# A dynamic convolution ahead of a feed-forward layer: its matmuls cut from 128 rows to two row halves of 64

## The chip, the cores and the metric

The kernel runs on one core of one Trainium2 chip. The metric is the device time of one execution in microseconds (us); less is better. A time is given as the median of several runs. The profile is of one further execution.

## The reference

```
B, S, D = 8, 4096, 192;  H, K = 8, 7;  group = D // H          # 24 channels a head
w = softmax(weight_gen, axis=-1)                               # [B, S, H, K]
x_pad = concatenate([zeros(B, K - 1, D), x], axis=1)
conv[b, s, h, g] = sum_k w[b, s, h, k] * x_pad[b, s + k, h, g] # causal, 7 taps, per token and head
h = maximum(conv.reshape(B * S, D) @ w_in, 0)                  # [32768, 192] @ [192, 2048]
out = (h * h) @ w_out                                          # [32768, 2048] @ [2048, 192], float32
```

Each token and head has seven weights of its own, which mix the token's row of `x` with the six rows before it. The result passes through a feed-forward layer with a squared ReLU.

## The kernel before, in words

**Tiling.** Tokens are taken in 64 subblocks of 512 (`TB`), eight to a batch. Subblocks are grouped in `BLOCKS`: the first two blocks have one subblock each, and all others two, which makes 33 blocks, numbered from 0. Two subblocks of a block are its two halves. The main loop (L858 to L893) runs over the blocks. In the loop for block j it computes the feed-forward layer's first matrix for block j, the second for the blocks before it, and the conv for block j + 1.

**Softmax.** Class `Softmax` (L190 to L279) turns `weight_gen` into normalized weights `v_big`, eight slots a token and head, of which seven hold the taps. `store` writes them to a DRAM tile `vd`. `wr_load` (L341) reads them back on SP's DMA queue, one row per input token of a conv piece, and `x_load` (L323) brings the rows of `x` on POOL's DMA queue. Both go through `block_load` (L307), in which a subblock has `NT` = 5 pieces of 128 input rows, one each `STEP` = 104 output tokens; the first and the last subblock of a batch part have a piece that is loaded on its own.

**Bands.** The conv is a matmul with a banded matrix. `st_bands` (L649) and `st_band` (L385) make it on VectorE: the row's weights `wr`, repeated, times a 0/1 `mask` (L115, made by POOL at the start) give `bd`, with 4160 elements a partition for a subblock.

**Conv.** From the ninth block on (`FIRST_SPREAD` = 8), `st_conv_spread` (L472) runs it. The result for 192 channels lies in `y` as slots of 64 partitions per half: each slot has two heads of 24 channels, at partitions 0 and 32 of the half, and in the remaining 8 partitions of each 32 a share of the last two heads. For four slots, five pieces, two halves and two heads of a slot it issues one matmul (L493): 128 input rows contract to 32 channels by 104 tokens (96 in the last piece). The 32 channels go to one of four column strips of the array (`tile_position=(0, p0)`), so that four matmuls in a row use four strips. That is 80 matmuls a block, into two PSUM tiles `yp`; ACT copies the first, VectorE the second to `y` (L503). The fourth slot (index `NK` = 3) holds the last two heads; four DMAs on SP (L507) move them into the free 8 partitions of the other slots. The conv before the ninth block is `st_conv` (L509, matmuls L527) or `st_conv_first` (L435).

**Feed-forward.** `st_unit` (L562) is one of 16 units of a block: three slots times two halves of 64 rows, in pairs, make `h` (L572); ACT applies the ReLU (L586), VectorE squares (L590). `st_mm2` (L602, matmul L621) multiplies with `w_o`, in pairs of 64 rows; ACT and VectorE add the two halves (`o_sum`, L635 and L637), and SP stores the rows (L642). `load_w_spread` (L143) puts the rows of `w_in` in the order in which the channels lie in `y`.

**Order.** The order on each engine is the program's order, written out by hand. A plan string per block sets it: for blocks whose successor is the ninth or a later one it is

```
steady_spread = "MuMuuu" * 2 + "MuCMuuu" + "MuMuuu"
```

with `u` a unit, `M` half a quarter of the second matrix, `C` the conv of the next block, followed by the `x` loads of the block after that. Bands for the next block are put at units 1 and 5. `h` and `yp` share a ring of three PSUM buffers (`ps_h`, two banks each). At the start (L689 to L733) POOL builds the mask (L692), issues loads, and clears `v_big` (L733); its next work is the `x` load of the fourth subblock and its share of the early `wr` loads (L355), which feed the bands for the first conv of L527.

Of the kernel before, what the change touches and what calls it, by code (L numbers as in the profile page):

```python
# [9 lines left out]
def kernel(  # L10
# [26 lines left out]
    nc = tc.nc  # L37
    f32 = mybir.dt.float32
    f16 = mybir.dt.float16

    B, S, D = x.shape
    H, KK = weight_gen.shape[2], weight_gen.shape[3]
# [3 lines left out]
    G = D // H  # L46
    SPREAD = H - 2
    FIRST_SPREAD = 8
    HP = H // 2

    P = 128
    TB = 512
    NBB = S // TB
    NSUB = B * NBB
    BLOCKS = [(0, 1), (1, 1)] + [(n, 2) for n in range(2, NSUB, 2)]
# [6 lines left out]
    SL = 8  # L62
    RT = 64
    NK = D // RT

    NT = 5
    STEP = 104
    BASE = -24
    starts = [BASE + STEP * i for i in range(NT)]
    bounds = [0, 104, 208, 312, 416, TB]  # L70
    ROW_ORDER = (0, 1, 2, 3, 4)

    AluOp = mybir.AluOpType
    AxisX = mybir.AxisListType.X
# [2 lines left out]
    const = ctx.enter_context(tc.tile_pool(name="const", bufs=1))  # L77
# [5 lines left out]
    p_bd = ctx.enter_context(tc.tile_pool(name="p_bd", bufs=3))  # L83
# [12 lines left out]
    w_p = const.tile([P, WQ, 2, NQ + NQ // 2], f16, name="w_p")  # L96
    w_o = const.tile([P, NF, Dm], f16, name="w_o")
    mask = const.tile([P, P, 2], f16, name="mask")
    FIRST = 8
    NSEL = TB + TB - P + FIRST - 1 + P  # L100
    sel = const.tile([P, NSEL], f16, name="sel")
    PARTS = {0: (8, 8, 8, 8), 1: (8, 8, 16), 2: (16, 16)}
    v_big = const.tile([P, R + 2 * HALO, HP, SL, 2], f16, name="v_big")
    v_first = [
        const.tile([P, FIRST + 2 * HALO, HP, SL, 2], f16, name=f"v_first{i}") for i in (0, 1)
    ]
# [18 lines left out]

    x_st = {}

    def load_w_in(dst, q, eng):  # L130
# [12 lines left out]
    def load_w_spread():  # L143

        def rows(head, k=None):
            a = moe_w_in[G * head : G * (head + 1)]
            return a if k is None else a.rearrange("(r k) c -> k r c", k=NK)[k]

        for e in (0, 1):
            for k in range(NK):  # L150
                for a, n, src in (
                    (0, G, rows(2 * k + e)), (G, RT // 2 - G, rows(SPREAD + e, k))
                ):
                    if k < 2:
                        p0 = RT * k + 32 * e + a
                        nc.gpsimd.dma_start(
                            out=w_p[p0 : p0 + n, :, 0, 0:NQ],
                            in_=src.rearrange("r (q c) -> r q c", q=WQ),
                        )
                    else:  # L160
                        for half in (0, 1):
                            p0 = RT * half + 32 * e + a
                            nc.gpsimd.dma_start(
                                out=w_p[p0 : p0 + n, :, 0, NQ:],
                                in_=src.rearrange("r (q h c) -> h r q c", q=WQ, h=2)[half],
                            )
# [23 lines left out]
    class Softmax:  # L190
# [35 lines left out]
        def exp(self, lo, hi):  # L226

            if lo == 0:
                self.ex = self.tile(p_one, p_one, "ex", HK, "ex8").rearrange(
                    "p (r g k e) -> p r g k e", g=HP, k=KK, e=2  # L230
                )
# [22 lines left out]
        def scale(self, lo, hi, eng):  # L254

            v = self.v
            while lo < hi:
                n = min(SL - lo % SL, hi - lo)
                for g in range(HP):
                    eng.tensor_tensor(  # L260
# [20 lines left out]
    vd_t = {}  # L281
# [7 lines left out]
    x_t, wr_t, pr_t, bd_t, yp_t, y_t, g_t, gp_t, t1_t, o_t, o_sb_t = ({} for _ in range(11))  # L289

    def rows(ap2d, t0, width):

        return bass.AP(
            tensor=ap2d.tensor, offset=ap2d.offset + t0 * width,
            ap=[[width, P], [STEP * width, NT], [1, width]],
        )
# [5 lines left out]
    def tile_start(j, i):  # L302

        t1 = (j % NBB + 1) * TB
        return TB - P if i == NT - 1 and t1 in ends(j // NBB) else starts[i]

    def block_load(j, dst, src, width, eng):  # L307
        t0 = (j % NBB) * TB
        first, last = int(t0 == 0), NT
        if first:  # L310
            eng.dma_start(out=dst[:, 0], in_=src[0:P, :])  # L311
        a = t0 + tile_start(j, NT - 1)
        if a != t0 + starts[-1]:
            last = NT - 1
            eng.dma_start(out=dst[:, last], in_=src[a : a + P, :])
        ap = rows(src, t0 + starts[first], width)
        ap = bass.AP(
            tensor=ap.tensor, offset=ap.offset,
            ap=[ap.ap[0], [STEP * width, last - first], ap.ap[2]],
        )  # L320
        eng.dma_start(out=dst[:, first:last], in_=ap)  # L321

    def x_load(j):  # L323
        x_t[j] = p_x.tile([P, NT, D], f16, name="xt")
        block_load(j, x_t[j], x[j // NBB], D, nc.gpsimd)

    def x_load_f32(j):
# [13 lines left out]
    def wr_load(j):  # L341
        wr_t[j] = p_wr.tile([P, NT, HP, SL * 2], f16, name="wr")
        wr = wr_t[j].rearrange("p t g c -> p t (g c)")
        block_load(j, wr, vd_t[j // NBB], H * SL, nc.sync)

    def wr_load_sbuf(j, parts, order, engines):
# [38 lines left out]
    def st_band(j, tiles):  # L385


        if j not in bd_t:
            bd_t[j] = p_bd.tile([P, H * NT * STEP], f16, name="bd")
        i = tiles[0]  # L390
        lo = STEP * i
        shift = 0 if i == 0 and j % NBB == 0 else lo - tile_start(j, i)
        n = min(STEP, P - shift)
        shape = (P, HP * len(tiles), n // SL, 2 * SL)
        nc.vector.tensor_tensor(  # L395
            out=bd_t[j][:, H * lo : H * (lo + len(tiles) * n)].rearrange(
                "p (g m c) -> p g m c", g=shape[1], c=2 * SL
            ),
            in0=wr_t[j][:, i : tiles[-1] + 1]
            .rearrange("p t g c -> p (t g) c")  # L400
            .unsqueeze(2)
            .broadcast_to(shape),
            in1=mask[:, shift : shift + n]
            .rearrange("p (m c) e -> p m (c e)", c=SL)
            .unsqueeze(1)
            .broadcast_to(shape),
            op=AluOp.mult,
        )

# [62 lines left out]
    def st_conv_spread(j):  # L472

        s0, n = BLOCKS[j]
        y = p_y.tile([P, NK + 1, TB], f16, name="y")
        y_t[j] = y
        for ks in ((NK, NK - 1), (0, 1)):
            yp = ps_h.tile([P, 2, TB], f32, name="yp", tag="h")
            k0 = min(ks)
            for k in ks:  # L480
                for i in range(NT):
                    a, b = bounds[i], bounds[i + 1]
                    for half in (0, 1):
                        s = s0 + half
                        hi = a + (STEP if tile_start(s, i) == starts[i] else b - a)
                        bd = bd_t[s][:, H * a : H * hi].rearrange(
                            "p (g c e) -> p g e c", g=HP, e=2
                        )
                        for e in (0, 1):
                            head = 2 * k + e  # L490
                            p0 = RT * half + 32 * e
                            c0 = min(G * head, D - 32)
                            nc.tensor.matmul(  # L493
                                out=yp[p0 : p0 + 32, k - k0, a:b],
                                lhsT=x_t[s][:, i, c0 : c0 + 32],
                                rhs=bd[:, head // 2, e, 0 : b - a],
                                start=True,
                                stop=True,
                                skip_group_check=True,
                                tile_position=(0, p0),  # L500
                            )
            copy = nc.vector.tensor_copy if k0 == 0 else nc.scalar.copy
            copy(out=y[:, k0 : k0 + 2], in_=yp)  # L503
        for p0 in range(0, P, 32):
            head = SPREAD + p0 // 32 % 2
            r0 = p0 + G * head - min(G * head, D - 32)
            nc.sync.dma_start(out=y[p0 + G : p0 + 32, 0:NK], in_=y[r0 : r0 + G, NK])  # L507

    def st_conv(j):  # L509

# [136 lines left out]
        )  # L647

    def st_bands(j):  # L649
        first = int(j % NBB == 0)  # L650
        last = NT - int(tile_start(j, NT - 1) != starts[-1])
        split = 2 if j == BLOCKS[NFIRST][0] else first
        for tiles in (range(first), range(first, split), range(split, last), range(last, NT)):
            if tiles:
                st_band(j, tiles)

    with nc.allow_low_precision("fp16 matmul pipeline"), tc.manual_schedule():
# [3 lines left out]
        for b in range(B):  # L661
            t0 = 0
# [68 lines left out]
        s2.load(nc.gpsimd)  # L731
        x_load(2)
        nc.gpsimd.memset(v_big, 0.0)  # L733

# [12 lines left out]
        fill = {}  # L749
# [22 lines left out]
        for n, s in enumerate(parts):  # L772
            k = n - min(m for m, p in enumerate(parts) if p.b == s.b)
# [4 lines left out]
        for n, s in enumerate(parts[4:], 4):  # L778
            b, f = s.b, s.fb
            k = n - min(m for m, p in enumerate(parts) if p.b == b)  # L780
# [8 lines left out]
        for j in range(len(plans), NBLK - 1):  # L789
            a = BLOCKS[j + 1][0]  # L790
# [67 lines left out]
        for j in range(NBLK):  # L858
# [6 lines left out]
            for step in plans[j].split():  # L865
                kind, n = step[0], int(step[1:] or 0)
# [29 lines left out]
        j = NBLK - 1  # L896
# [44 lines left out]
```

The softmax here doesn't subtract the row's maximum and nothing guards it: scores larger than these inputs give would overflow.

## Time and profile before

| what | us |
|---|---|
| median of three runs | 732.07 (731.87 to 732.11) |
| the profiled execution | 731.82 |
| its span, from the first to the last instruction | 730.0 |
| PE, matmuls busy | 724.1 |
| VectorE busy | 626.8 |
| ACT busy | 612.2 |
| POOL busy | 99.8 |
| the conv matmuls of L493, 2000 of them, in 25 convs | first at 155.2, last at 686.4 |

The granted TensorE clock is 1.0 through the whole span. Shares in the profile are of the span. A group's row gives the line, the engine, the operation, what is written from what, the shapes (partitions x elements), the count, then busy us and mean ns of one, and the idle time before them with what ended it. Matmuls overlap one another, so their busy times say less than the distance of their starts.

### The profile page before, as it was taken

The numbers are of one execution on the slowest core, as the hardware profiler recorded it, in microseconds if no ns is written. First come the engines' busy times: TensorE is split into PE (matmuls) and PEld (weight loads), VectorE is DVE, ScalarE is ACT, GpSimd is POOL, SyncE is SP. The second block draws the span as 40 slices with busy tenths as digits, with TensorE's granted clock in tenths as the row PEclk, the third lists the DMA queues.
The fourth block names the chain that finished last, engine by engine and source line by source line (L and its number), as shares of the span: only waits on it lengthen the run. The fifth ranks groups of instructions, "written<-read, shape, count | busy, mean of one in ns | idle before, by whom it ended". The sixth has DMA issues, their size and how long they took to land.

```text
span 730.0 us, 30988 instructions
## 1 busy us (share of the span) xinstructions
PE 724.1 (99%) x14053; PEld 528.0 (72%) x14053; DVE 626.8 (86%) x836; ACT 612.2 (84%) x733; POOL 99.8 (14%) x145
## 2 busy tenths in 40 slices
PE   8999999999999999999999999999999999999998
PEld 4657788777777777777777777777777777777777
DVE  7998998998898988888988888988889988778753
ACT  5999888888888888888888888888888888888883
POOL 8131223321001100011001010010000110001000
PEclk9999999999999999999999999999999999999999
DMA  9555455685345452455432554343544325444012
GB/s 202 118 105 115 82 96 105 132 149 129 86 66 138 90 92 59 82 117 124 76 64 61 136 104 88 56 77 116 107 84 86 57 52 119 66 87 78 30 45 68
DMA packets 125984, 68.30 MB, mean 94 GB/s; under 512 B 85321, under 2 KB 122140, under 8 KB 125340
## 3 DMA queue, kind: packets, MB, share of 16 engines
q0 software_dynamic: 46192, 19.43, 22.9%
q1 hardware_dynamic: 79516, 46.79, 22.4%
q8 instruction: 110, 1.80, 1.1%
q14 instruction: 22, 0.18, 0.1%
q10 hardware_dynamic: 144, 0.10, 0.0%
HBM read 50.18 MB, written 28.70 MB: 108 GB/s over the span
## 4 chain that ended last, share of the span: by engine, by line
PE 98%; ACT 1%; DVE 0%; DMA 0%; issue 0%
PE o L621 47%; PE h L572 44%; PE yp L493 4%; PE h L557 2%; PE yp L527 1%; DMA wg<-in_weight_gen_dram 0%; PE yp L455 0%; ACT y L538 0%; DVE v_first L260 0%; PE pr L372 0%; ACT t L586 0%; DVE ssum L245 0%; ACT ex L238 0%; DVE rcp L252 0%; ACT wr L381 0%
## 5 line engine op out<-in xcount | busy, mean ns | idle before, releaser
L586 ACT ACTIVATE t<-h 128x1024 f16<-128x1024 f32 x512 | 496.4, 1026 | 60.3 <-PE h L572 58.8
L621 PEld LDWEIGHTS <-g 64*128 64x128 f16 (+1 forms) x8032 | 344.3, 94 | 55.0 <-issue 2.2
L621 PE MATMUL o<-w_o,g 64*128 64x192 f16 (+1 forms) x8032 | 380.1, 243 | 0.1
L590 DVE TENSOR_TENSOR g<-t 128x2048 f16<-128x2048 f16 (+1 forms) x287 | 307.4, 1105 | 30.1 <-ACT t L586 29.9
L572 PE MATMUL h<-y,w_p 64*128 64x512 f16 x2400 | 291.7, 376 | 0.0
L572 PEld LDWEIGHTS <-w_p 64*128 64x128 f16 x2400 | 113.9, 94 | 94.7
L395 DVE TENSOR_TENSOR bd<-wr,mask 128x4160 f16<-128x4160 f16 (+4 forms) x90 | 149.6, 1686 | 1.3 <-ACT wr L381 0.7
L637 DVE TENSOR_TENSOR o_sb<-o,o_sb 128x384 f32<-128x384 f32 x123 | 68.4, 556 | 61.1 <-ACT o_sb L635 60.1
L321 POOL DMA_DIRECT2D xt<-in_x_dram x63 | 52.6, 839 | 415.3 <-PE yp L493 362.5
L635 ACT COPY o_sb<-o 128x384 f32<-128x384 f32 x129 | 61.6, 477 | 45.9 <-PE o L621 45.1
L572 PE MATMUL h<-y,w_i 64*128 64x512 f16 x576 | 70.6, 376 | 0.3 <-ACT t L586 0.3
L572 PEld LDWEIGHTS <-w_i 64*128 64x128 f16 x576 | 30.3, 94 | 22.2 <-issue 1.6
L493 PEld LDWEIGHTS <-xt 128*32 128x32 f16 x2000 | 24.6, 95 | 10.6 <-issue 10.6
L260 DVE TENSOR_TENSOR v_big<-ex,rcp 128x112 f16<-128x112 f32 (+5 forms) x180 | 29.9, 237 | 1.7 <-DMA vd<-v_big 0.7
L503 DVE CAST y<-yp 128x1024 f16<-128x1024 f32 x25 | 30.4, 1218 | 0.0
L493 PE MATMUL yp<-bd,xt 128*32 128x104 f16 (+1 forms) x2000 | 28.4, 210 | 0.0
L238 ACT ACTIVATE ex<-wg 128x560 f32<-128x560 f32 (+4 forms) x38 | 25.9, 682 | 1.9 <-DMA wg<-in_weight_gen_dram 1.9
L245 DVE TENSOR_REDUCE ssum<-ex 128x80 f32<-128x560 f32 (+4 forms) x38 | 25.3, 666 | 1.3 <-ACT ex L238 1.3
L503 ACT CAST y<-yp 128x1024 f16<-128x1024 f32 x25 | 25.2, 1007 | 0.0
L252 DVE RECIPROCAL rcp<-ssum 128x80 f32<-128x80 f32 (+4 forms) x38 | 22.8, 600 | 1.3
L311 POOL DMA_DIRECT2D xt<-in_x_dram x7 | 3.9, 554 | 120.9 <-PE yp L493 109.4
L355 POOL DMA_DIRECT2D wr<-v_first x24 | 12.9, 560 | 25.1 <-DVE v_first L260 13.6
(41 smaller groups left out, 115.1 us busy)
## 6 DMA issues: line engine op xcount, KB each, us to landing
out_dram<-o_sb SPq DMA_DIRECT2D x63, 384.0 KB
xt<-in_x_dram POOLq DMA_DIRECT2D x42, 240.0 KB, 4.7
wg<-in_weight_gen_dram SPq DMA_DIRECT2D x4, 1064.0 KB
xt<-in_x_dram POOLq DMA_DIRECT2D x21, 192.0 KB, 5.2
wr<-vd SPq DMA_DIRECT2D x38, 80.0 KB
vd<-v_big SPq DMA_DIRECT2D x5, 512.0 KB
y<-y SPq DMA_DIRECT2D x100, 24.0 KB
wg<-in_weight_gen_dram SPq DMA_DIRECT2D x3, 616.0 KB
```

What stands on the lines that cost most here:

```text
L238: nc.scalar.activation(out=self.ex[:, lo:hi].rearrange("p r g k e -> p (r g) k e"), in_=self.wg[:, lo:hi].rearrange("p r (g e) k -> p (r g ...
L260: eng.tensor_tensor(out=bass.AP(tensor=v.tensor, offset=v.offset + lo * H * SL + lo % SL * 2 + g * SL * 2, ap=[list(v.ap[0]), [H * SL + 2, ...
L321: eng.dma_start(out=dst[:, first:last], in_=ap)
L395: nc.vector.tensor_tensor(out=bd_t[j][:, H * lo : H * (lo + len(tiles) * n)].rearrange("p (g m c) -> p g m c", g=shape[1], c=2 * SL), in0= ...
L493: nc.tensor.matmul(out=yp[p0 : p0 + 32, k - k0, a:b], lhsT=x_t[s][:, i, c0 : c0 + 32], rhs=bd[:, head // 2, e, 0 : b - a], start=True, sto ...
L503: copy(out=y[:, k0 : k0 + 2], in_=yp)
L572: nc.tensor.matmul(out=h[:, half], lhsT=w_in_chunk(w, u, slot, half), rhs=y_t[j][r0 : r0 + RT, k], start=(slot == 0), stop=(slot == NK - 1 ...
L586: nc.scalar.activation(out=t1[:, e], in_=h, func=ActF.Relu)
L590: nc.vector.tensor_tensor(out=g[:, a : e + 1], in0=t1[:, a : e + 1], in1=t1[:, a : e + 1], op=AluOp.mult)
L621: nc.tensor.matmul(out=oo[:, cc * Dm : (cc + 1) * Dm], lhsT=g[r0 : r0 + n, cc * P : (cc + 1) * P], rhs=w_o[r0 : r0 + n, fc, :], start=(fc ...
L635: nc.scalar.copy(out=o_sb, in_=o[0][:, c])
L637: nc.vector.tensor_tensor(out=o_sb, in0=o[1][:, c], in1=o_sb, op=AluOp.add)
```

## The change

From the ninth block on, which is from subblock 14 on (`FIRST_HALF`), the conv works on pieces of 64 input rows (`RT`) instead of 128. A subblock is cut into two halves of 256 tokens (`HT`), and each half into five pieces of 64 rows, 56 tokens apart (`HSTEP`). Row half 0 of the array takes the pieces of the first 256 tokens, row half 1 those of the second. A matmul contracts 64 rows to 32 channels by 56 tokens (32 in the first piece). Two row halves and four column strips make eight positions; each row half writes a PSUM bank of its own, and the copies to `y` put the columns back in order. 160 matmuls make a block's conv.

`x_load` and `wr_load` take these subblocks through `half_load`: two DMAs each, of 64 partitions, and at a batch's start a memset and one more DMA for `wr`. The band is one VectorE operation of 2240 elements (`st_band_half`), with a mask of its own, which POOL makes at the start, after it has cleared `v_big`. The second head of a slot now lies at partition 8 of its 32, so that the free partitions of both heads adjoin and the fourth slot is moved by two DMAs of 16 partitions instead of four of 8. `load_w_spread` follows that order with as many DMAs as before.

```diff
+    HT = TB // 2
+    HSTEP = RT - SL
+    HBASE = HT - RT - (NT - 1) * HSTEP
+    FIRST_HALF = BLOCKS[FIRST_SPREAD][0]
...
+    def band_mask_half():
+
+        nc.gpsimd.memset(mask_h, 1.0)
+        for r0 in (0, RT):
+            for sign, base in ((1, SL), (-1, KK - 1 - SL)):
+                nc.gpsimd.affine_select(
+                    out=mask_h[r0 : r0 + RT], in_=mask_h[r0 : r0 + RT],
+                    pattern=[[sign, HSTEP], [0, 2]], compare_op=AluOp.is_ge,
+                    fill=0.0, base=base, channel_multiplier=-sign,
+                )
...
+    def half_load(j, dst, src, width, eng, before):
+
+        for n, r0 in enumerate((0, RT)):
+            t0 = (j % NBB) * TB + HT * n + HBASE
+            first = int(t0 < 0 and not before)
+            if first:
+                nc.vector.memset(dst[0:-t0, 0], 0.0)
+                eng.dma_start(out=dst[-t0:RT, 0], in_=src[0 : RT + t0])
+            eng.dma_start(
+                out=dst[r0 : r0 + RT, first:],
+                in_=bass.AP(
+                    tensor=src.tensor, offset=src.offset + (t0 + first * HSTEP) * width,
+                    ap=[[width, RT], [HSTEP * width, NT - first], [1, width]],
+                ),
+            )
...
+    def st_band_half(j):
+
+        bd_t[j] = p_bd.tile([P, H * NT * STEP], f16, name="bd")
+        shape = (P, HP * NT, HSTEP // SL, 2 * SL)
+        nc.vector.tensor_tensor(
+            out=bd_t[j][:, 0 : H * NT * HSTEP].rearrange(
+                "p (g m c) -> p g m c", g=shape[1], c=2 * SL
+            ),
+            in0=wr_t[j].rearrange("p t g c -> p (t g) c").unsqueeze(2).broadcast_to(shape),
+            in1=mask_h.rearrange("p (m c) e -> p m (c e)", c=SL).unsqueeze(1).broadcast_to(shape),
+            op=AluOp.mult,
+        )
...
                 for i in range(NT):
-                    a, b = bounds[i], bounds[i + 1]
+                    t0 = HBASE + HSTEP * i
+                    a, b = max(t0 + SL, 0), t0 + RT
                     for half in (0, 1):
                         s = s0 + half
...
                         for e in (0, 1):
-                            head = 2 * k + e
+                            head = 2 * k + (e if k < NK else 1 - e)
                             p0 = RT * half + 32 * e
-                            c0 = min(G * head, D - 32)
-                            nc.tensor.matmul(
-                                out=yp[p0 : p0 + 32, k - k0, a:b],
-                                lhsT=x_t[s][:, i, c0 : c0 + 32],
-                                rhs=bd[:, head // 2, e, 0 : b - a],
-                                start=True,
-                                stop=True,
-                                skip_group_check=True,
-                                tile_position=(0, p0),
-                            )
+                            c0 = G * head - (SP8 if head % 2 else 0)
+                            for n, r0 in enumerate((0, RT)):
+                                nc.tensor.matmul(
+                                    out=yp[p0 : p0 + 32, n, (k - k0) * HT :][:, a:b],
+                                    lhsT=x_t[s][r0 : r0 + RT, i, c0 : c0 + 32],
+                                    rhs=bd[r0 : r0 + RT, i, head // 2, head % 2, HSTEP - (b - a) :],
+                                    start=True,
+                                    stop=True,
+                                    skip_group_check=True,
+                                    tile_position=(r0, p0),
+                                )
             copy = nc.vector.tensor_copy if k0 == 0 else nc.scalar.copy
-            copy(out=y[:, k0 : k0 + 2], in_=yp)
-        for p0 in range(0, P, 32):
-            head = SPREAD + p0 // 32 % 2
-            r0 = p0 + G * head - min(G * head, D - 32)
-            nc.sync.dma_start(out=y[p0 + G : p0 + 32, 0:NK], in_=y[r0 : r0 + G, NK])
+            copy(
+                out=y[:, k0 : k0 + 2].rearrange("p k (n c) -> p n k c", c=HT),
+                in_=yp.rearrange("p n (k c) -> p n k c", c=HT),
+            )
+        for r0 in (0, RT):
+            nc.sync.dma_start(
+                out=y[r0 + G : r0 + RT - G, 0:NK], in_=y[r0 + SP8 : r0 + RT - SP8, NK]
+            )
...
         nc.gpsimd.memset(v_big, 0.0)
+        band_mask_half()
```

More of the change, by code (lines that the diff above doesn't have):

```diff
@@ L49 @@
     HP = H // 2
+    SP8 = 32 - G
     P = 128
@@ L98 @@
     mask = const.tile([P, P, 2], f16, name="mask")
+    mask_h = const.tile([P, HSTEP, 2], f16, name="mask_h")
     FIRST = 8
@@ L150, in load_w_spread @@
             for k in range(NK):
+                own = SP8 * e
                 for a, n, src in (
-                    (0, G, rows(2 * k + e)), (G, RT // 2 - G, rows(SPREAD + e, k))
+                    (own, G, rows(2 * k + e)), ((own + G) % 32, SP8, rows(H - 1 - e, k))
                 ):
@@ L321, in block_load @@
         eng.dma_start(out=dst[:, first:last], in_=ap)
+    def half_load(j, dst, src, width, eng, before):
[12 more added lines that the diff above has]
+            )
     def x_load(j):
         x_t[j] = p_x.tile([P, NT, D], f16, name="xt")
+        if j >= FIRST_HALF:
+            return half_load(j, x_t[j], x[j // NBB], D, nc.gpsimd, True)
         block_load(j, x_t[j], x[j // NBB], D, nc.gpsimd)
@@ L343, in wr_load @@
         wr = wr_t[j].rearrange("p t g c -> p t (g c)")
+        if j >= FIRST_HALF:
+            return half_load(j, wr, vd_t[j // NBB], H * SL, nc.sync, False)
         block_load(j, wr, vd_t[j // NBB], H * SL, nc.sync)
@@ L481, in st_conv_spread @@
                 for i in range(NT):
-                    a, b = bounds[i], bounds[i + 1]
+                    t0 = HBASE + HSTEP * i
+                    a, b = max(t0 + SL, 0), t0 + RT
                     for half in (0, 1):
                         s = s0 + half
-                        hi = a + (STEP if tile_start(s, i) == starts[i] else b - a)
-                        bd = bd_t[s][:, H * a : H * hi].rearrange(
-                            "p (g c e) -> p g e c", g=HP, e=2
+                        bd = bd_t[s][:, 0 : H * NT * HSTEP].rearrange(
+                            "p (t g c e) -> p t g e c", t=NT, g=HP, e=2
@@ L649, in st_bands @@
     def st_bands(j):
+        if j >= FIRST_HALF:
+            return st_band_half(j)
         first = int(j % NBB == 0)
```

## The prediction

> **What bounds the kernel now.** I read the page first: the busy shares, and the chain that ended last.
>
> ```profile
> PE 724.1 (99%) x14053; PEld 528.0 (72%) x14053; DVE 626.8 (86%) x836; ACT 612.2 (84%) x733; POOL 99.8 (14%) x145
> ...
> PE 98%; ACT 1%; DVE 0%; DMA 0%; issue 0%
> PE o L621 47%; PE h L572 44%; PE yp L493 4%; PE h L557 2%; PE yp L527 1%; DMA wg<-in_weight_gen_dram 0%; PE yp L455 0%; ACT y L538 0%; DVE v_first L260 0%; PE pr L372 0%; ACT t L586 0%; DVE ssum L245 0%; ACT ex L238 0%; DVE rcp L252 0%; ACT wr L381 0%
> ```
>
> TensorE is the whole path, and the lines that change (L493) hold 4% of it. Busy shares of a pipelined engine can deceive, so I asked next for the waits from 155 to 690 us, where the changed conv runs.
>
> ```profile
> POOL xt L321 <- PE yp L493: 362.5, 18, 20.4
> ...
> ACT t L586 <- PE h L572: 48.2, 173, 0.4
> ...
> ACT o_sb L635 <- PE o L621: 32.4, 93, 0.6
> ...
> PEld L493 <- issue: 10.6, 25, 0.4
> ```
>
> Everybody waits for TensorE and TensorE for nobody: its one row is the gap of 0.4 us ahead of each conv's first weight load. Last, the chain of waits around one conv, in order of time (start, length, what).
>
> ```profile
> 504.89 1.94 PE h L572 x18
> 506.83 1.32 PE o L621 x32
> 508.15 0.65 PE h L572 x6
> 508.80 1.05 PE yp L493 x75
> 509.85 1.43 PE o L621 x32
> 511.28 1.94 PE h L572 x18
> ```
>
> A block is 48 pairs of `h` (1.94 us for 9 pairs, 215.6 ns each), eight steps of `o` (1.32 us for 16 pairs, 82.5 ns each), and one conv. The conv's row is 1.05 us, and the step of `o` after it takes 0.11 us more than the others. So a conv costs 1.16 us, and 16 x 0.647 + 8 x 1.32 + 1.16 = 22.1 us is the period of the blocks (486.71 to 508.80 in the chain). There are 25 such convs: 29 us.
>
> Inside the conv I took the start of every matmul, averaged over the 25. The 80 matmuls come in 20 groups of four, 3 ns apart in a fresh group; groups start at 0, 59, 106, 154, 201 ns and so on: 48 ns a group of 104 columns, 44 to 45 ns one of 96, 11 ns extra once. From first to last start are 931 ns. Around that lie 90 ns at the entry (306 ns instead of 216 after the last `h` pair) and 137 ns from the last start to the first `o`.
>
> [...] the 64-row pairs of `h` and `o` start 3 ns apart and stream together. No run here shows eight 64x32 tiles.
>
> **The change, part by part.** *Conv matmuls.* 20 groups of four at 104 or 96 columns become 20 groups of eight at 56 columns (one piece in five: 32). The price of a column: (215.6 - 82.5) / (512 - 192) = 0.416 ns, and 2.6 ns per matmul. That gives 45.9 ns at 104 columns where the conv shows 48, so the small tiles add 2.1 ns. For 56 columns: 23.3 + 2.6 + 2.1 = 28 ns. Issue is close to it: a load and its matmul start 3.3 ns apart in a burst, eight pairs take 27 ns, so I take 28 for the 32-column groups too. Below, 25.9 ns (the bare line) is the bound; above, 35 ns if starts and streams don't mesh. [...] First to last start is then 19 x 28 + 11 + 7 x 3.3 = 566 ns for 931: 365 ns less. The exit has 40 fewer columns to stream: 17 ns less. [...] Sum: 0.38 us x 25 = **9.5 us off the path**.
>
> *Bands.* The two common shapes give the rate:
>
> ```profile
> L395 DVE TENSOR_TENSOR bd<-wr,mask 128x4160 f16<-128x4160 f16 x41 | 94.9, 2316 | 0.1
> L395 DVE TENSOR_TENSOR bd<-wr,mask 128x3328 f16<-128x3328 f16 x21 | 39.6, 1884 | 0.1
> ```
>
> (2316 - 1884) / 832 = 0.52 ns an element, so 2240 elements cost 1.32 us; 50 subblocks save some 50 us of VectorE. It is off the path, worth nothing directly. Six memsets of 32 rows are added there; nothing.
>
> *Loads.* From the diff, 50 subblocks issue 100 `xt` loads for 64 on POOL, and 106 `wr` loads for 64 on SP; the two-transfer move of the fourth slot makes 50 of 100 on SP, at 0.67 us each. The rows moved are as many. POOL sits idle 20 us per block behind the conv, so its extra 0.5 us is hidden; if it weren't, it would still have to grow by over 10 us before the next conv, 22 us later, saw it. SP queues its stores and `wr` loads behind the move, 1.3 us earlier than now; nothing waits there longer.
>
> *Copies out of PSUM* keep their sizes (1.01 us ACT, 1.22 us VectorE).
>
> *The half mask* is new on POOL: a memset and four selects over 224 elements, queued after L733. The two selects of the full mask (256 elements) took 2.54 us, so four take about 4.4 us, plus 0.3. Behind them stand, once:
>
> ```profile
> 14.86 2.49 POOL L733 MEMSET v_big<- 128x2816 f16 x1
> 17.70 0.58 POOL L315 DMA_DIRECT2D xt<-in_x_dram  x1 [0.34 <-PE yp L455]
> 18.26 0.75 POOL L321 DMA_DIRECT2D xt<-in_x_dram  x1
> 22.52 2.72 POOL L355 DMA_DIRECT2D wr<-v_first  x5 [3.50 <-DVE v_first L260]
> ...
> 27.46 3.73 DVE L395 TENSOR_TENSOR bd<-wr,mask 128x2496 f16<-128x2496 f16 x3 [0.33 <-DMA wr<-v_first]
> ```
>
> POOL ends the masks at 22.0, the two `xt` issues at 23.3, and the five `wr` issues slip 0.8 us. The band at 27.46 waits for such a landing, and its row ends at 31.19, when the conv of L527 starts (31.20). Only the last piece needs the last band, so I let 0.3 us of slip pass: **0.5 us onto the path**, once; from 0 (another landing was the late one) to 2 us (the `xt` transfer in front holds up the landing).
>
> **Sum.** The profiled execution took 731.82 us (span 730.0, 1.8 around it). 731.82 - 9.5 + 0.5 = 722.8; the median of the runs stands 0.25 above it: **723.0 us**.
>
> **Rivals.** *A, slower: the supply of instructions.* A conv becomes 320 PE instructions for 160, in 0.57 us for 0.93. [...] The trace shows no more than 160 in 0.93 us, 172 per us. [...] Against it speaks the first conv, where PE stood at a semaphore until 9.73:
>
> ```profile
> 9.76 0.23 PEld L455 LDWEIGHTS <-xt 128*32 128x32 f16 x16 [0.25 <-ACT wr L381]
> ```
>
> The first load starts at 9.757, and the eighth, the 15th instruction, at 9.811: at least 259 per us, with TensorE's own streams in the way. Chance 0.10.
>
> *B, slower: it isn't eight at once.* If two row tiles of a column strip run in turn, a group takes 56 ns, and a conv 19 x 56 + 39 - 931 = 0.17 us more, less 0.02: +3.8 + 0.5, 736 us. The pairs of `h` and `o` speak against it. Chance 0.06.
>
> *C, no change: a wait takes the gain's place.* Units after the conv reuse the PSUM buffers that the copies empty. The busy times in one block, in us, for PE, weight loads, VectorE, ACT and POOL (then clock, DMA share, GB/s):
>
> ```profile
> 486.60:508.70 22.10, 22.10 (x434) 16.13 (x432) 19.93 (x29) 18.83 (x22) 2.16 (x3) 1.00 0.50 114
> ```
>
> ACT is busy 18.83 of 22.10 us and VectorE 19.93, which falls by 2. The third unit after the conv needs VectorE's copy, which now ends 0.8 us ahead of it; 0.4 remain, more with VectorE relieved. If each block gave back its 0.38 us, the time is 732 us. Chance 0.09, with what I have overlooked.
>
> **Numbers.** The forecast's case has 0.75, with its milder form of A (725 to 730). Its own range: 719.5 [...] to 729 (35 ns a group, 2 us early). The range reaches on to C, 733; A and B, 0.16, are left out. A change of 0.2% (1.5 us) is about what a measurement of this kernel can tell from none: faster 0.75, same 0.09, slower 0.16.
>
> **What would show it.** In the chain: L493 near 0.67 us instead of 1.05, the next `o` still near 1.4, the period near 21.7 us. Starts of 28 ns a group, eight in each. [...] B as 56 ns from the first group; C as PE rows in the waits. The early cost shows as the start of L527's first conv, 31.7 for 31.20. I am wrong if the period grows, or if L493's row shrinks and the period doesn't.

## The result and the profile after

The changed kernel takes 783.33 us (median of four runs, 781.76 to 784.43) against 732.09 us before: a ratio of 1.0698, 95% interval 1.0682 to 1.0714. The forecast was 723.0 us, faster. It is slower by 51.2 us, outside the range that the forecast gave.

The page of the changed kernel: busy time of each engine, the chain that ended last by engine, and the queue that the profile calls "instruction" (packets, MB, share).

```profile
PE 739.1 (94%) x16053; PEld 543.1 (69%) x16053; DVE 583.1 (75%) x828; ACT 612.6 (78%) x733; POOL 120.6 (15%) x186
...
q8 instruction: 125, 2.05, 1.1%
...
PE 90%; issue 5%; DMA 0%; ACT 0%; DVE 0%; DVEq 0%
```

TensorE is still the path, but no longer all of it: 5% of the chain is "issue", time in which an engine waits for nothing that the profile shows. Before, that share was 0%. The waits from 155 us on say where it stands (who waited for whom, total us, times, longest; L546 is the conv's matmul, L677 that of `o`, L628 that of `h`):

```profile
ACT o_sb L691 <- PE o L677: 80.1, 93, 3.3
...
PEld L546 <- issue: 50.8, 50, 1.9
...
PE yp L546 <- issue: 37.5, 25, 1.8
```

ACT waits for TensorE longer than before (80.1 us for 32.4), so it is not what holds the kernel. TensorE itself is idle for 1.5 us on average in each of the 25 convs, and no semaphore, no other engine and no transfer of data is named. The chain around one conv, in order of time:

```profile
491.01 1.32 PE o L677 x32
492.33 0.65 PE h L628 x6
492.98 1.31 PE yp L546 x144
494.29 1.50 issue
495.79 0.24 PE yp L546 x13
496.03 1.43 PE o L677 x32
```

Around this conv `h` and `o` take what they took. The conv takes 1.31 + 1.50 + 0.24 = 3.05 us in place of 1.05, and is broken in two. The period of the blocks, from the first start of one conv to that of the next, was 22.093 us on average and is 24.148 us: 2.055 us x 25 = 51.4 us. That is the whole loss; everything else nearly cancels.

One block of the profile holds something more. From 545.6 to 549.0 us, close behind a stall, the granted clock is 0.5, and `o` and `h` take longer there:

```profile
542.72 1.81 issue
544.77 1.89 PE o L677 x32
546.66 3.15 PE h L628 x18
```

This block is 1.7 us longer than one with an equal stall. Two stalls as long, in the convs at 372.4 and 639.2 us, have no such stretch behind them; what decides stays open.

The starts of the conv's matmuls, averaged over the 25 convs (first of each group of eight, in ns; behind the stall, the rest of group 19, and group 20), show two things:

```
group     1    2    3    4    5    6    7    8   ...   18    19 | stall | rest, 20
start     0   39   65   94  213  279  346  413  ... 1105  1172 | 1.69 us | 2882, 2899
```

The first four groups, 32 matmuls with their 32 weight loads, start 27 to 29 ns apart (39 once, at the beginning), as forecast. Then comes a gap of 85 ns ahead of matmul 33. From the fifth group on a group takes 66.7 ns, which is 8.33 ns for a load and its matmul; only the fourteenth takes 92 ns, also without a stall in the conv. And after matmul 147, always that one, the next matmul starts only 1.3 to 2.0 us later.

Of the rivals, A (the supply of instructions) fits the first: a burst of 64 instructions, then a slower pace. For the second I formed this theory: instructions come in portions of 256, pages from here on, and the conv uses a page up faster than the next one comes. The trace has 125 packets of the "instruction" queue, 16,384 bytes each, for 32,115 PE records, which are 257 a packet. And the stall's place counts out: among all PE records of the trace, loads, matmuls and a few semaphore instructions, it comes after number 193 modulo 256 (193 left over when the number is divided by 256), in each of the 25 convs. A block has 96 + 256 + 160 matmuls, each with a load: 1024 instructions, four pages exactly, so the boundary falls on the same matmul in each. The packets fit in time, too: in each of the 25 convs one begins 0.1 to 0.9 us behind the conv's start, and the stall ends 1.2 to 1.5 us after that packet does. The time that a page needs to come is an estimate from this trace: if the supply is ahead by the 64 instructions of the burst, it begins the conv's page 3 pairs of `h` (0.65 us) and 7 matmuls of `o` (0.29 us) ahead of the conv, some 0.9 us, and TensorE goes on 2.45 to 3.19 us into it, 2.88 on average; so 3.4 to 4.1 us, 3.8 on average. The rivals that remained: the stall belongs to the conv (a buffer, the tiling, the half loads), or the row halves don't mesh (B).

### The profile page after: what moved, and what is told of

Same layout as the page of the kernel before. It is cut to its first block, busy times and chain, and to the rows that moved or that the text cites. A ratio compares the mean times of both kernels' runs of the same rounds, so it can differ in the third digit from the quotient of the medians.

```text
span 782.6 us, 35001 instructions
## 1 busy us (share of the span) xinstructions
PE 739.1 (94%) x16053; PEld 543.1 (69%) x16053; DVE 583.1 (75%) x828; ACT 612.6 (78%) x733; POOL 120.6 (15%) x186
## 4 chain that ended last, share of the span: by engine, by line
PE 90%; issue 5%; DMA 0%; ACT 0%; DVE 0%; DVEq 0%
PE o L677 43%; PE h L628 41%; PE yp L546 5%; PE yp L583 1%; DMA wr<-v_first 0%; DVE bd L434 0%; ACT y L594 0%; ACT t L642 0%; PE h L613 0%; ACT o_sb L691 0%; DVEq L434 0%
## 5 line engine op out<-in xcount | busy, mean ns | idle before, releaser
L677 PEld LDWEIGHTS <-g 64*128 64x128 f16 (+1 forms) x8032 | 345.6, 94 | 53.3 <-issue 2.9
L677 PE MATMUL o<-w_o,g 64*128 64x192 f16 (+1 forms) x8032 | 381.2, 243 | 0.5 <-issue 0.5
L646 DVE TENSOR_TENSOR g<-t 128x2048 f16<-128x2048 f16 (+1 forms) x287 | 311.5, 1106 | 34.2 <-ACT t L642 29.3
L628 PE MATMUL h<-y,w_p 64*128 64x512 f16 x2400 | 292.9, 377 | 0.0
L628 PEld LDWEIGHTS <-w_p 64*128 64x128 f16 x2400 | 114.2, 94 | 95.7 <-issue 1.6
L350 POOL DMA_DIRECT2D xt<-in_x_dram x100 | 66.5, 684 | 514.8 <-PE yp L546 504.1
L546 PE MATMUL yp<-bd,xt 64*32 64x56 f16 (+1 forms) x4000 | 40.6, 190 | 37.5 <-issue 37.5
L628 PE MATMUL h<-y,w_i 64*128 64x512 f16 x576 | 71.2, 376 | 0.3 <-ACT t L642 0.3
L546 PEld LDWEIGHTS <-xt 64*32 64x32 f16 x4000 | 35.2, 89 | 50.8 <-issue 50.8
L453 DVE TENSOR_TENSOR bd<-wr,mask_h 128x2240 f16<-128x2240 f16 x50 | 65.8, 1316 | 1.6 <-DMA wr<-vd 1.6
L628 PEld LDWEIGHTS <-w_i 64*128 64x128 f16 x576 | 33.4, 94 | 19.7 <-issue 1.6
L434 DVE TENSOR_TENSOR bd<-wr,mask 128x3328 f16<-128x3328 f16 (+5 forms) x26 | 33.2, 1311 | 1.8 <-DMA wr<-v_first 0.9
L340 POOL DMA_DIRECT2D xt<-in_x_dram x13 | 10.9, 841 | 42.4 <-PE yp L583 42.4
```

The source lines that it names most:

```text
L350: eng.dma_start(out=dst[r0 : r0 + RT, first:], in_=bass.AP(tensor=src.tensor, offset=src.offset + (t0 + first * HSTEP) * width, ap=[[width ...
L434: nc.vector.tensor_tensor(out=bd_t[j][:, H * lo : H * (lo + len(tiles) * n)].rearrange("p (g m c) -> p g m c", g=shape[1], c=2 * SL), in0= ...
L453: nc.vector.tensor_tensor(out=bd_t[j][:, 0 : H * NT * HSTEP].rearrange("p (g m c) -> p g m c", g=shape[1], c=2 * SL), in0=wr_t[j].rearrang ...
L546: nc.tensor.matmul(out=yp[p0 : p0 + 32, n, (k - k0) * HT :][:, a:b], lhsT=x_t[s][r0 : r0 + RT, i, c0 : c0 + 32], rhs=bd[r0 : r0 + RT, i, h ...
L628: nc.tensor.matmul(out=h[:, half], lhsT=w_in_chunk(w, u, slot, half), rhs=y_t[j][r0 : r0 + RT, k], start=(slot == 0), stop=(slot == NK - 1 ...
L646: nc.vector.tensor_tensor(out=g[:, a : e + 1], in0=t1[:, a : e + 1], in1=t1[:, a : e + 1], op=AluOp.mult)
```

## The experiments

**Moving the boundary.** Nothing of the conv is touched; more, shorter warm-up matmuls at the start shift all later instructions against the pages.

```diff
-                nc.tensor.matmul(out=wp, lhsT=warm[:, 0:P], rhs=warm, start=True, stop=True)
+                nc.tensor.matmul(
+                    out=wp[:, 0:128], lhsT=warm[:, 0:P], rhs=warm[:, 0:128], start=True, stop=True
+                )
...
-        spin(21)
+        spin(84)
```

> The changed kernel, with the 21 warm-up matmuls of 512 columns at the start made into 84 of 128 columns: as many columns, 126 more PE instructions ahead of everything. Theory (instruction supply in pages of 256): the stall after pair 147 of each conv sits on a boundary of 256 instructions; now the boundary falls after pair 84, with the page before it begun some 4.7 us ahead of the conv, and a fetch that needs about 3.8 us is in time. The stall of 1.7 us goes in all 25 convs: 783.3 - 42 = 741 us, range 737 to 746, and the pairs keep 8.3 ns. Rival (the stall belongs to the conv itself: a buffer, a transfer, the tiling): still after pair 147, 783 us.

Measured: 742.31 us, ratio to before 1.0145 (1.0128 to 1.0162). The stall is gone; only the first conv still has a short one, of 0.16 us. The chain:

```profile
514.97 0.65 PE h L628 x6
515.62 1.42 PE yp L546 x156
517.04 1.43 PE o L677 x32
518.47 1.94 PE h L628 x18
```

The conv is one piece of 1.42 us, from first to last start 1303 ns on average, and the pairs keep 8.33 ns. The period is 22.453 us.

> The changed kernel with 53 warm-up matmuls of 204 columns for 21 of 512: 64 more PE instructions ahead. Theory (pages of 256 instructions, about 3.8 us from the beginning of a page to the next one's being there): the boundary moves to pair 115, the page before it begins 2.7 us ahead of the conv, the next page is there 1.1 us into it, and the conv needs it at 0.8: a stall of 0.3 us after pair 115; 783.3 - 25 x 1.35 = 750 us, range 744 to 760. Rival (the stall belongs to the conv itself): after pair 147, 783 us.

53 warm-up matmuls of 204 columns. Measured: 758.12 us (one run). In most convs the stall comes after matmul 115, where it was forecast, 32 pairs earlier for 64 instructions more. The conv's first to last start took 1917 ns on average: the stall averages 0.6 us instead of 0.3, and varies between nothing and 1.2 us. It is short where the packet ends early: here too TensorE goes on 1.2 to 1.5 us behind the packet's end, wherever it stands for 0.4 us or more. So the place was right, and the time that a page needs was taken as too short and too steady.

```profile
479.95 1.05 PE yp L546 x113
481.00 0.73 issue
481.73 0.52 PE yp L546 x42
482.25 1.43 PE o L677 x32
```

> The changed kernel with 133 warm-up matmuls of 80 columns for 21 of 512: 224 more PE instructions ahead. Theory (pages of 256): boundaries after pair 35 and 3 pairs behind the conv's end. The page that begins at pair 35 is used up in about 1.4 us, and its successor needs 3.8: the stall leaves the conv and stands 3 pairs behind its end, 2.5 us long; 783.3 + 25 x 0.8 = 803 us, range 793 to 812. Rival (the stall belongs to the conv itself): after pair 147, 783 us.

133 warm-up matmuls of 80 columns. Measured: 800.41 us (one run). The conv is whole again, 1300 ns, and TensorE stops three matmuls behind it, in `o`, in 25 of 25 blocks, 2.1 us from one matmul's start to the next:

```profile
504.28 1.42 PE yp L546 x155
505.70 0.27 PE o L677 x3
505.97 1.77 issue
507.74 1.41 PE o L677 x29
```

In shift64 and shift224 the stalls again stand after PE record 193 modulo 256. A wait that can be moved out of the conv by more and shorter warm-up matmuls hundreds of us earlier belongs to the instruction stream, not to the conv. These three runs decide it. Part of the time of shift224 isn't in the stalls themselves: its granted clock is 0.5 in four stretches of 3.4 us behind stalls, where the change has one.

**What sets 8.33 ns a pair.** Both on top of shift126. First, every matmul of the conv streams 112 columns (short of the edges, neighbouring columns are taken along):

```diff
+                                wide, a2 = 2 * HSTEP, min(a, HT - 2 * HSTEP)
+                                off = min((i * HP + head // 2) * wide, (NT * HP - 2) * wide)
...
-                                    out=yp[p0 : p0 + 32, n, (k - k0) * HT :][:, a:b],
+                                    out=yp[p0 : p0 + 32, n, (k - k0) * HT :][:, a2 : a2 + wide],
...
-                                    rhs=bd[r0 : r0 + RT, i, head // 2, head % 2, HSTEP - (b - a) :],
+                                    rhs=bd_t[s][r0 : r0 + RT, off : off + 2 * wide].rearrange(
+                                        "p (c e) -> p e c", e=2
+                                    )[:, head % 2],
```

> As shift126, with every conv matmul streaming 112 columns instead of 56 or 32, part of them columns of another piece, so that the conv computed is not the reference's. Theory (dispatch of one instruction in 4.17 ns is the limit inside the conv): 66.7 ns a group of eight stays, since 112 columns need 51 ns; within 3 us of shift126. Rival (the streams of eight tiles set the pace, as 66.7 ns a group): a group grows by 23 ns or more, 20 groups and 25 convs, at least 11.5 us more than shift126.

Measured: 744.28 us (1.0155 to 1.0185), 2.0 us above shift126, part of it from a later start (its first such conv begins 1.5 us later). The conv grew by 44 ns on average, 36 of them in its first four groups, the first three of which now take 51 to 62 ns; from the fifth on a group is 66.7 ns again. Twice the columns and more cost nothing where the pace is 66.7 ns.

> As shift126, with the conv's loops turned so that four matmuls of one row half come together and then four of the other. Theory (dispatch): as many instructions, a group of four streams in 28 ns and is dispatched in 33, so the conv takes as long as in shift126; within 2 us of it. Rival (eight tiles at once are worth their concurrency): turned loops cost 40 groups at 28 or more instead of 20, and the conv gets longer than 1.24 us only if concurrency counts; 5 us or more above shift126.

```diff
-                    for half in (0, 1):
-                        s = s0 + half
...
-                        for e in (0, 1):
...
-                            for n, r0 in enumerate((0, RT)):
+                    for n, r0 in enumerate((0, RT)):
+                        for half in (0, 1):
...
+                            for e in (0, 1):
```

Measured: 743.03 us (1.0138 to 1.0174), and a conv of 1311 ns for 1303. Whether eight or four tiles come one after another makes no difference. Rival B, too, is out: the first groups of eight start 27 to 29 ns apart.

**The number of instructions alone.** The kernel before, 128 rows, four strips, full loads and the old move; each conv matmul is merely issued as two of half the columns.

```diff
-                    for half in (0, 1):
+                    for part, half in ((0, 0), (0, 1), (1, 0), (1, 1)):
...
+                        lo_c, hi_c = (b - a) // 2 * part, (b - a) // 2 * (part + 1)
...
-                                out=yp[p0 : p0 + 32, k - k0, a:b],
+                                out=yp[p0 : p0 + 32, k - k0, a + lo_c : a + hi_c],
...
-                                rhs=bd[:, head // 2, e, 0 : b - a],
+                                rhs=bd[:, head // 2, e, lo_c:hi_c],
```

> The kernel before, with nothing of the change but the number of instructions: each conv matmul of 104 or 96 columns from the ninth block on is issued as two of 52 or 48, 128 rows as before, four column strips. Theory (instruction supply alone): 160 pairs at the same place in the instruction stream; 8.3 ns a pair after a first burst, and the stall of 1.7 us after pair 147; 782 us, range 776 to 788. Rival (row halves, loads in halves or the early mask are the cause): 40 groups of 26 ns, 1.05 us for 0.93, 735 us.

Measured: 788.05 us (one run), 5 us more than the change. Three more stretches at half the clock behind stalls (four for one in the change's profile), at 1.7 us each as estimated from the block above, are about that much.

```profile
475.92 0.65 PE h L573 x6
476.57 1.26 PE yp L494 x139
477.83 1.85 issue
479.68 0.32 PE yp L494 x21
479.99 1.43 PE o L622 x32
```

The first 32 pairs run at 25.4 ns a group of four, then a pair takes 8.33 ns, then comes the stall: the picture of the change without the change. The stall starts at pair 147 and comes half a pair earlier with each block, down to pair 134: here a block has 1025 PE instructions, one more than four pages.

> The kernel before with each conv matmul of the ninth block and later issued as two of half the columns, and with the 84 warm-up matmuls of 128 columns of shift126: the instruction count of the change at the harmless place, nothing else of it. Theory (instruction supply is the whole cause): 8.3 ns a pair after the first 32 pairs and no stall, 25 convs of 1.30 us for 0.93, less 0.02 at the exit, plus 1 us at the start; 741 to 743 us, as shift126. Rival (part of shift126's 10 us comes from row halves, half loads or the move in two transfers): under 739 us.

Measured: 746.23 us (1.0184 to 1.0212), 3 us above the forecast. The convs are as forecast, 1312 ns each, none broken, and the first eight periods are 22.46 us, as with the change. The rest are new stalls: in nine of the later blocks TensorE stops behind the conv, 2.1 to 2.5 us after its last matmul starts, for up to 0.8 us from one start to the next. All nine stand after record 193 modulo 256 again. The boundary drifts here, and I take it that a page with a conv in it is used up too soon for the boundary behind the conv as well. The forecast counted only boundaries inside.

> The kernel before with the 84 warm-up matmuls of 128 columns alone. Theory: a page boundary that shift126 showed in the row selection at 12.3 us costs 0.6 to 0.9 us once, and nothing later, since a conv of 160 instructions uses no page up in under 3.8 us; 732.5 to 733.2 us. Rival (the boundary's place matters to short convs too): 735 us or more.

Measured: 732.66 us, ratio 1.0010 (1.0003 to 1.0016), 20 runs. The stall is in the row selection near 12.3 us, 1.0 us of "issue"; with 0.6 us more in all, the runs show no further cost of the boundary's place in the convs of 160 instructions.

**The mask at the start.**

> The kernel before with the half mask built on POOL at the start, and not used. Theory: POOL's share of the early loads slips by some 0.4 to 0.8 us, a band waits for it, and the first conv of L527 comes up to 0.6 us later; 0.0 to 0.6 us above before. Rival (the slip is hidden): no difference to be measured.

Measured: 732.25 us, ratio 1.0003 (0.9995 to 1.0011): no difference. In its profile the masks take POOL until 21.0 us and its `wr` loads start at 22.72 for 22.52; no band waits for them.

> As shift126, with the half mask built in block 5 on POOL instead of at the start. Theory: the first conv of the old form starts at 31.2 again instead of 31.5, doesn't stop halfway for a band, and about 0.7 to 1.0 us go; 0.3 to 1.3 us below shift126. Rival (the early microsecond has another cause, such as the warm-up): no difference.

Measured: 744.30 us (1.0145 to 1.0194), 2.0 us above shift126, where 0.3 to 1.3 below was forecast. Why it is longer stays open, and of the mask this run can't tell: in both, the page stall at 12.3 us (0.91 us of "issue" in shift126, 0.86 here) has made TensorE late already, and no band waits in either.

## Why the prediction was wrong, point by point

- **What bounds the kernel**: right. TensorE is the path before and after; what the sum lacked is the time in which TensorE itself has no instruction.
- **Conv matmuls, "eight pairs take 27 ns, so I take 28"**: the step that failed first. I took the pace of a burst for a pace that lasts. It held for four groups, 32 pairs; then 8.33 ns a pair against the 3.5 of a group of 28 ns. Without a stall the conv takes 1303 ns from first to last start (shift126) where I had 566, and 931 were to be beaten. Period against period this is 22.453 - 22.093 = 0.36 us, x 25 = 9 us lost where 9.5 were to be gained.
- **Rival A** named that mechanism, and I gave it 0.10. What is there at once, the burst shows: 32 loads and 32 matmuls. The pace of the rest was read wrongly: the first conv's 14 instructions in 54 ns gave "at least 259 per us", and 240 are sustained (one in 4.17 ns; 14 take 58 ns). Of the eight loads there, the last seven start 3 to 5 ns apart, which is the pace of a burst (3.3 ns in the changed conv). I take it that they were waiting already; then their starts say nothing of how fast new ones come. Worse, with the 64 of the burst a conv of 320 needs 256 more, and to fit them into the old 931 ns takes 275 per us; 259 lies below that, so it never spoke against A.
- **What no case held**: the page, the larger of the two steps that failed, put at nothing. 24.148 - 22.453 = 1.695 us a block, 42.4 of the 51.4 us, the one stretch at half the clock in it. The trace of before had 110 packets of 16,384 bytes, but no wait for them: from 155 to 690 us the longest time from one PE record's start to the next is 305 ns, at the convs' entry. I take it that a page there lasts longer than the 3.4 to 4.1 us that its successor needs by the estimate above. The changed conv takes 256 instructions in 1.07 us, at 4.17 ns each.
- **The exit**, 17 ns less: 121 ns for 137. **Bands**: 1.32 us forecast, 1.316 measured; VectorE's busy time fell by 44 us for some 50 forecast, and it was worth nothing, as said. **Loads and the move in two transfers**: hidden, as said; no wait on TensorE names them, and before_halved, without them, shows the same convs.
- **The early 0.5 us**: not confirmed. In the changed kernel's profile a band waits 0.85 us for a `wr` landing, and the first conv of L583 is late and broken, 0.65 us in all; with the mask alone (before_mask) neither the profile nor the times show any of it. Four selects took 3.3 us for my 4.4. What made that landing late in that execution stays open.
- **Rival C**: no engine's wait took the gain's place; TensorE's row of waits names only "issue".

The shown causes are two: the pace of 8.33 ns a pair, for 160 more instructions (9 us), and the page stall (42 us). That the pace is one of single instructions is the reading that fits best: loads and matmuls start alternately, one each 4.17 ns. But every matmul here has a load of its own, so a limit on pairs or on loads isn't ruled out. What makes the gap of 85 ns ahead of pair 33 stays open. No version here beats the kernel before: at 4.17 ns an instruction its conv of 160 would need 667 ns, less than the 931 that it takes, and by the same estimate the 256 instructions behind the burst in a conv of 320 need 1.07 us, wherever the pages fall.

## What to carry to other kernels

The smaller tiles doubled the conv's instructions here, 320 for 160, and without a stall the conv took 1303 ns for 931. Before splitting matmuls, count the instructions of the stage and hold them against a rate that a trace shows sustained (here 240 per us), not against the gaps of a burst (here 3.3 ns a pair, for 32 pairs); where a stage issues hundreds in about a microsecond, as the 320 here, look for page stalls too. Where the profile puts a wait down to "issue", always at the same instruction number modulo 256 (here 193, in 25 of 25 convs), suspect the supply of instructions: shifting the stream by some dummy instructions, as here, tells in one run whether the wait moves with the stream or stays with the work.

## What the runs showed of the hardware

- After 32 load-and-matmul pairs that start 3.3 ns apart (64x32 tiles) or 6.4 ns (128x32), PE takes 8.33 ns a pair, with both tiles, at 32, 48, 52, 56 and 112 columns. Pair 33 started 213 ns after the first where the burst's last matmul started at 128 (the change), and at 224 where it started at 202 (before_halved).
- In the kernel before, from 155 to 690 us, no two PE records in a row start more than 305 ns apart; in the changed one TensorE stands 1.3 to 2.0 us at the second of the two boundaries of 256 PE records that fall into each conv. The packet of 16,384 bytes at that place takes 0.9 to 1.6 us, about 1.2 on average, and TensorE goes on 1.2 to 1.5 us after its end.
- The same change cost 10 us or 68 us (shift126, shift224) by the number of warm-up instructions at the start.
